# An explicit, state-free inverse of each 64-step triangle in an RWKV-7 and MLP kernel

## The chip, the cores and the metric

The kernel runs on one core of a Trainium2 chip. The metric is the device time of one execution in microseconds. All arithmetic is fp32.

## What is computed

An attention block with a recurrent state (RWKV-7) for 4 sequences, 8 heads, 768 steps and a head dimension of 40, followed by an MLP with a quick GELU on the 3072 resulting rows of 320 numbers. The reference, cut to what matters:

```python
for t in range(S):                                   # S = 768
    y[:, :, t] = einsum('bhd,bhde->bhe', r_t, state)
    Sa = einsum('bhde,bhe->bhd', state, a_t)
    state = state * w_t[:, :, None, :] - einsum('bhd,bhe->bhde', Sa, b_t) + einsum('bhd,bhe->bhde', v_t, k_t)
x = y.transpose(0, 2, 1, 3).reshape(3072, 320)
h = x @ w_in                                         # 320 x 2048
out = (h * sigmoid(1.702 * h)) @ w_out               # 2048 x 320
```

The kernel doesn't walk the steps. It takes 64 steps (a chunk) at once. Within a chunk, Sa at each step depends on Sa at the earlier steps of the chunk, which is a linear system with a unit triangular 64 x 64 matrix for each sequence and head: (I - N) X = B. N comes from a, b and the decay w alone; B has a part from v and k (A times v) and a part from the state that enters the chunk.

## The kernel before

**Units.** The work is cut into 24 units, numbered i: chunk c = i // 2 of twelve, and p = i % 2, a pair of sequences. A unit holds 2 sequences x 8 heads, so 16 triangles, eight on each half of the 128 partitions. Every product is made of four 64 x 64 tiles that run beside each other on the four quarters of TensorE (QUARTERS, helper mm at line 271, which is therefore the line of every matmul in the profile). An mm is two MATMUL and two LDWEIGHTS records.

**What happens in a unit.** decay (L476) makes the factors FT, GT and G from sums of log w. prep (L524) multiplies a, b and k by them and forms three score matrices: score_NT (L541, the transpose of N, masked to the upper triangle by L549), score_A (L554, masked by L562) and, times v, Av (L566, L574); score_RV (L578) is the same for r and v. solve (L605) then makes z, the decayed entering state (L614), and score_N (L618), whose product holds N (64 columns) and the state's part of B (40 columns) side by side; L630 masks the one, L633 adds Av to the other. Both go into the tile W, so from here on each step carries the state.

**The levels.** level (L665) is called for n = 0 to 5 and each of two halves b. For the late units (i of 4 and more) it runs Newton-like steps with a correction matrix E: the product has 104 columns (N and X), and for NT 64 more, and VectorE makes E (L707, L721, L716) while ScalarE or VectorE copies the product into the next W (L726). At the first level L705 subtracts from a tile called edge, which aside (L658) fills. The first four units (EARLY) use plain squaring, with an extra product by the identity in each level, and need E only at the end. The last level gives X for the tile M. sa_turned (L733) gives its transpose saT. The first two units have no entering state.

**The rest of a unit.** scores (L759) and read (L771) form the output y and the new state zraw (L788), which the unit i + 2 needs for its z. y is multiplied by FT (L812), goes to DRAM (L822) and comes back as xT (L826).

**MLP.** mlp (L834) has for each chunk 16 x 5 up tasks of 256 columns, a gelu on ScalarE for each pair of blocks (L847) and two times 8 down tasks of 320 columns. The weights arrive as float64 and are decoded to fp32 on VectorE and ScalarE by weight (L369 to L418) in eight pieces, in the first part of the run.

**What sets the order.** Everything is a task with a rank, a list of engines that can run it with a price for each, and the tiles that it reads, writes or needs room for. The class Plan (L59) orders all tasks ahead of time by a simulation with these prices: at each moment a free engine takes the task of lowest rank that is ready. Attention ranks by unit (10 i and about), weights have RANKS from 14 to 41, the MLP 10000 and more, so MLP products fill what attention leaves free on TensorE. The engines tried first are PE, ACT, DVE, POOL, in that order. Once written, the order on each engine is fixed. PSUM is four pairs of banks, and up and down hold at most one pair each. ak, b, W and E have two buffers, so one for each p.

Of the kernel before, what the change touches and what calls it, by code (L numbers as in the profile page):

```python
# [224 lines left out]
def rwkv7_gelu_quick(ctx: ExitStack, tc: tile.TileContext, time_d, v_d, w_d, wc_d, ak_d, b_d, rv_d, w_in, w_out, out):  # L225
# [11 lines left out]
    LEVELS = 6  # L237
# [13 lines left out]
    plan = Plan(dict(logw=3, wc=3, G=1, wch=3, wz=2, time=2, ak=2, b=2, rv=2, FT=3, GT=1, kh=2, bh=2, bz=2,  # L251
                     A=1, Av=1, RV=2, W=2, W0=2, W1=2, E=2, E0=2, E1=2, edge=1, zraw=2, zT=1, saT=1, M=2, y=1, x=1, xT=3, g=4, ob=1), 4)
# [72 lines left out]
    edge = single("edge", [128, 2, 2, 2, 168])  # L325
    for b, j in product(BITS, BITS):
        nc.vector.tensor_copy(edge[:, :, b, j, :64], ident.unsqueeze(1).to_broadcast([128, 2, 64]))
        nc.vector.tensor_copy(edge[:, :, b, j, 104:], ident.unsqueeze(1).to_broadcast([128, 2, 64]))
    twice = single("twice", [128, 64])
    nc.vector.tensor_add(twice, ident, ident)  # L330
# [14 lines left out]

    W_t, E_t = several("W", [128, 2, 2, 2, 168]), several("E", [128, 2, 2, 2, 128])

    ak_t, b_t, rv_t = several("ak", [128, 2, 8, 64]), several("b", [128, 8, 64]), several("rv", [128, 2, 8, 64])
    bz_t = several("bz", [128, 8 * 104 + 24])
    for t in bz_t:  # L350
        nc.gpsimd.memset(t[:, 8 * 104:], 0.0)
# [161 lines left out]
    Av_of = lambda i: buf("Av", i, [128, 2, 2, 2 * D])  # L513
    W_of = lambda s: W_t[s % 2]
    E_of = lambda s: E_t[s % 2]
# [6 lines left out]
    bz_of = lambda i: bz_t[i % 2][:, :8 * 104].rearrange("p (j n) -> p j n", n=104)  # L522

    def prep(i):  # L524
# [8 lines left out]
            bz_of(i)[:, :, :64], in0=b_of(i), scalar=-1.0, in1=GT_of(i), op0=ALU.mult, op1=ALU.mult),  # L533
                 reads=T("b", "GT"), writes=T("bz", "bhT"))
# [6 lines left out]
        def score_NT(t):  # L541

            ps = psum(t, "ps_NT")
            for b, f in product(BITS, BITS):
                for e, u in QUARTERS:
                    o, j = (2 * b + f) * 64, slot(b, u, f)
                    mm(ps[HALF[u], e, o:o + 64], bz_of(i)[HALF[e], j, :64], ahT()[HALF[e], j], o == 0)
        plan.add(R + 1, pe((4, 64)), score_NT, reads=T("bhT", "ahT"), uses=T("bz", "ak"), room=halves("W", first_w(i)), pair=("NT", i))
        plan.add(R + 1, dve(512), lambda t: nc.vector.tensor_tensor(  # L549
            W_of(first_w(i)).rearrange("p e b f n -> p e (b f) n")[:, :, :, 104:],  # L550
            psum(t, "")[:, :, :256].rearrange("p e (j t) -> p e j t", t=64), mask(upper), ALU.mult),
                 writes=halves("W", first_w(i)), pair=("NT", i))

        def score_A(t):  # L554

            ps = psum(t, "ps_A")
            for u, f in product(BITS, BITS):
                for e, b in QUARTERS:
                    o, j = (2 * u + f) * 64, slot(b, u, f)
                    mm(ps[HALF[b], e, o:o + 64], khT()[HALF[e], j], ahT()[HALF[e], j], o == 0)  # L560
# [5 lines left out]
        def times_v(t):  # L566

            ps, v_b = psum(t, "ps_Av"), time_of(i)[:, 2]
            for e, f in product(BITS, BITS):
                for b, u in QUARTERS:  # L570
                    o, h = (2 * e + f) * D, head(e, f, b, u)
                    mm(ps[HALF[u], b, o:o + D], A_of(i)[HALF[b], 4 * e + 2 * u + f], v_b[HALF[b], h * D:(h + 1) * D], o == 0)
        plan.add(R + 1, pe((4, 40)), times_v, reads=T("A", "time"), room=T("Av"), pair=("Av", i))
        plan.add(R + 1, any2(320), lambda t: copy(t.engine)(  # L574
            Av_of(i).rearrange("p e b n -> p b e n"), psum(t, "")[:, :, :160].rearrange("p b (e n) -> p b e n", e=2)),
# [18 lines left out]
    def first_w(i):  # L594
        return 2 * LEVELS * (i // 2) + i % 2

    def last_e(i):

        k, early = i // 2, EARLY // 2
        return 2 * (min(k, early - 1) + (LEVELS - 1) * max(k - early + 1, 0)) + i % 2  # L600

    def halves(name, n):
        return [(f"{name}{b}", n) for b in BITS]

    def solve(i):  # L605
# [4 lines left out]
        Av = lambda: Av_of(i).rearrange("p e b (f d) -> p e (b f) d", f=2)  # L610
        first = lambda: W_of(first_w(i)).rearrange("p e b f n -> p e (b f) n")

        if c > 0:
            plan.add(R, {"DVE": 490.0, "sbuf": True}, lambda t: nc.vector.tensor_mul(  # L614
                bz_of(i)[:, :, 64:], zraw_of(i - 2), wz_of(i).unsqueeze(2).to_broadcast([128, 8, D])),
                     reads=[("zraw", i - 2), ("wz", i)], writes=T("bz", "z"))

        def score_N(t):  # L618

            ps, n = psum(t, "ps_N"), 104 if c > 0 else 64  # L620
            for b, f in product(BITS, BITS):
                for e, u in QUARTERS:
                    o, j = (2 * b + f) * 104, slot(b, u, f)
                    mm(ps[HALF[u], e, o:o + n], ahT()[HALF[e], j], bz_of(i)[HALF[e], j, :n], o == 0)
        plan.add(R, pe((4, 104)), score_N, reads=T("ahT", "bhT", "Av") + (T("z") if c > 0 else []), uses=T("ak", "bz"),
                 room=halves("W", first_w(i)), pair=("N", i))

        def get(t):
            return psum(t, "")[:, :, :416].rearrange("p e (j n) -> p e j n", n=104)
        plan.add(R, dve(512), lambda t: nc.vector.tensor_tensor(first()[:, :, :, :64], get(t)[:, :, :, :64], mask(lower), ALU.mult),  # L630
                 writes=halves("W", first_w(i)), pair=("N", i))
        if c > 0:
            plan.add(R, dve(320), lambda t: nc.vector.tensor_add(first()[:, :, :, 64:104], get(t)[:, :, :, 64:], Av()),  # L633
                     reads=T("Av"), writes=halves("W", first_w(i)) + [("X", i)], pair=("N", i))

            def state_turned(t):

                ps, bz = psum(t, "ps_zT"), bz_t[i % 2]
                for u, b in product(BITS, BITS):
                    for e, f in QUARTERS:  # L640
                        o, at = (2 * u + b) * D, slot(b, u, f) * 104 + 64
                        mm(ps[HALF[f], e, o:o + D], bz[HALF[e], at:at + 64], ident[HALF[e], :D], o == 0)
            plan.add(R + 5, pe((4, 40)), state_turned, reads=T("z", "bhT"), uses=T("bz"), room=T("zT"), pair=("zT", i))
            plan.add(R + 5, any2(320), lambda t: copy(t.engine)(
                zT_of(i)[:, :DM].rearrange("p (r n) -> p r n", r=2), psum(t, "")[:, :, :160]), writes=T("zT"), pair=("zT", i))
        else:
            plan.add(R, any2(320), lambda t: copy(t.engine)(first()[:, :, :, 64:104], Av()), reads=T("Av"), writes=halves("W", first_w(i)))

        def signed(t, dst, src, done=False):

            if done:
                copy(t.engine)(dst, src)
            elif t.engine == "ACT":
# [4 lines left out]
        def aside(t):  # L658

            for u, e in QUARTERS:  # L660
                signed(t, edge[HALF[e], u, :, :, 64:104], W_of(first_w(i))[HALF[u], e, :, :, 64:104])
        if i >= EARLY:
            plan.add(R + 1, {"ACT": 4 * 330.0, "DVE": 4 * 330.0, "sbuf": True}, aside, reads=[("X", i)], uses=halves("W", first_w(i)), writes=T("edge"))

        def level(n, b):  # L665

            last = n == LEVELS - 1  # L670
            early = i < EARLY
            alone = n == 0 or early and not last
            s, es = first_w(i) + 2 * n, last_e(i) + 2 * (n - LEVELS + 1 if i >= EARLY else 0 if last else -1)

            def go(t):
                w, ps = W_of(s)[:, :, b], psum(t, "ps_level")
                E = None if alone else E_of(es)[:, :, b]
                lo = 0 if n < LEVELS - 2 else 64
                for j in BITS:
                    o = j * 208  # L680
                    for h, q in QUARTERS:
                        mm(ps[HALF[q], h, o + lo:o + 104], E[HALF[h], q, j, 64:] if E else w[HALF[h], q, j, 104:],
                           w[HALF[h], q, j, lo:104], j == 0)
                    if not last:
                        for h, q in QUARTERS:
                            mm(ps[HALF[q], h, o + 104:o + 168], E[HALF[h], q, j, :64] if E else w[HALF[h], q, j, :64],
                               w[HALF[h], q, j, 104:], False)
                if early and alone:
# [40 lines left out]
        for n in range(LEVELS):  # L729
            for b in BITS:  # L730
                level(n, b)
# [260 lines left out]
```

## Time and profile before

The median of three runs is 823.99 us (822.45 to 827.14). The profiled execution has a span of 816.7 us.

| operation | busy, us | instructions |
|---|---|---|
| ps_level products, by tile | 224 | 8768 MATMUL |
| up products | 274 | 3840 MATMUL |
| down products | 244 | 3072 MATMUL |
| y products | 42 | 1536 MATMUL |
| VectorE on level results (L705, L707, L716, L721, L726) | 189 | 292 |
| ScalarE copies W (L726) | 102 | 164 |

A tile's busy time counts the moments in which at least one of its matmuls was in flight. Matmuls of different tiles overlap, so the times of tiles add up to more than TensorE's busy time. The table of groups gives mean durations of single instructions[...]; the chain of work that ended last gives stretches from start to start and is the better place to read what a piece of TensorE work costs. [...]

### The profile page before, as it was taken

To read this page: it belongs to the slowest core of one execution; us is meant where nothing else is said; L and a number is where in the kernel's file an instruction comes from. 1 tells how busy PE (TensorE), PEld (TensorE's weight loads), DVE (VectorE), ACT (ScalarE), POOL (GpSimd) and SP (SyncE) were. 2 spreads that over 40 slices of the span, in tenths; PEclk is the share of its full clock that TensorE was granted. 3 is DMA by queue.
4 is the path that set the end of the run, shared out by engine and by line. 5 is a ranking of instruction groups with operands and counts; after the bars stand their busy time and mean duration, and the time that the engine had idled before them with its cause. 6 is when DMAs were issued, how large, how long until landed. Compare 5 with 4: busy or idle time off the path is not lost.

```text
span 816.7 us, 51357 instructions
## 1 busy us (share of the span) xinstructions
PE 749.6 (92%) x24192; PEld 636.1 (78%) x24192; DVE 477.7 (58%) x764; ACT 352.3 (43%) x603; POOL 153.3 (19%) x209
## 2 busy tenths in 40 slices
PE   4567887999999999999999989999999999999997
PEld 3556766787798888788888888887787887899785
DVE  7489778755755755756755654745556545455200
ACT  4376874444344253245254344355346345243210
POOL 4024052012202302302302302302103213200000
PEclk9899999999999999999999999999999999999999
DMA  9834452223403502412412512412403213110200
GB/s 348 329 110 146 136 194 72 70 69 89 134 17 91 152 20 86 133 45 82 138 45 68 152 44 74 141 46 72 142 15 98 71 50 92 40 33 4 60 10 18
DMA packets 32731, 76.31 MB, mean 93 GB/s; under 512 B 5096, under 2 KB 14312, under 8 KB 31496
## 3 DMA queue, kind: packets, MB, share of 16 engines
q1 hardware_dynamic: 32520, 73.03, 28.7%
q8 instruction: 190, 3.11, 1.6%
q14 instruction: 21, 0.17, 0.1%
HBM read 65.14 MB, written 7.86 MB: 89 GB/s over the span
## 4 chain that ended last, share of the span: by engine, by line
PE 79%; ACT 7%; DVE 6%; issue 4%; DMA 3%; SPq 1%; POOL 0%; ACTq 0%; DVEq 0%; POOLq 0%
PE ps_down L271 24%; PE ps_up L271 22%; PE ps_level L271 17%; PE ps_y L271 4%; PE ps_N L271 2%; ACT W L726 2%; PE ps_saT L271 1%; PE ps_Av L271 1%; PE ps_M L271 1%; PE ps_NT L271 1%; PE ps_A L271 1%; PE ps_RV L271 1%; PE ps_rz L271 1%; ACT L847 1%; PE ps_zT L271 1%
## 5 line engine op out<-in xcount | busy, mean ns | idle before, releaser
L271 PE MATMUL ps_up<-xT,w_sb 64*64 64x256 f32 x3840 | 274.5, 378 | 7.6 <-issue 4.5
L271 PE MATMUL ps_down<-w_sb,g 64*64 64x320 f32 x3072 | 243.8, 431 | 2.9 <-DVE w_sb L406 1.6
L726 ACT COPY W<-ps_level 128x672 f32<-128x672 f32 (+1 forms) x164 | 102.4, 626 | 184.2 <-PE ps_level L271 176.7
L271 PEld LDWEIGHTS ps_up<-xT,w_sb 64*64 64x64 f32 x3840 | 159.9, 134 | 27.3 <-issue 7.2
L271 PEld LDWEIGHTS ps_level<-W,E 64*64 64x64 f32 x5888 | 153.0, 134 | 27.9 <-issue 4.5
L271 PEld LDWEIGHTS ps_down<-w_sb,g 64*64 64x64 f32 x3072 | 130.9, 133 | 43.8 <-DVE w_sb L406 2.0
L271 PE MATMUL ps_level<-W,E 64*64 64x64 f32 (+2 forms) x5888 | 152.2, 230 | 7.8 <-issue 2.5
L721 DVE TENSOR_TENSOR E<-twice,ps_level 128x512 f32<-128x512 f32 x120 | 81.8, 686 | 87.8 <-ACT W L726 75.6
L538 POOL TENSOR_TENSOR kh<-time,G 128x320 f32<-128x320 f32 x23 | 20.8, 906 | 414.5 <-issue 289.3
L271 PE MATMUL ps_level<-W 64*64 64x64 f32 (+2 forms) x2560 | 69.4, 239 | 22.1 <-issue 10.3
L271 PEld LDWEIGHTS ps_level<-W 64*64 64x64 f32 x2560 | 66.2, 138 | 29.5 <-issue 15.0
L847 ACT ACTIVATE g<-ps_up 128x1024 f32<-128x1024 f32 x48 | 49.2, 1026 | 42.6 <-PE ps_up L271 42.2
L812 POOL TENSOR_TENSOR x<-y,FT 128x128 f32<-128x128 f32 x88 | 56.1, 667 | 0.7 <-DVE y L802 0.4
L705 DVE TENSOR_TENSOR W<-edge,ps_level 128x672 f32<-128x672 f32 x40 | 33.9, 850 | 12.2 <-PE ps_level L271 11.1
L530 POOL TENSOR_TENSOR ak<-ak,FT 128x512 f32<-128x512 f32 x20 | 27.9, 1394 | 64.1 <-DMA ak<-in_ak 55.8
L873 DVE TENSOR_TENSOR ob<-ob,ps_down 128x320 f32<-128x320 f32 x24 | 11.6, 482 | 48.0 <-ACT ob L871 45.7
L271 PE MATMUL ps_y<-RV,kh 64*64 64x104 f32 x768 | 37.1, 251 | 1.3 <-issue 1.3
L271 PE MATMUL ps_y<-M,bh 64*64 64x104 f32 x768 | 37.5, 250 | 0.5 <-issue 0.4
L726 DVE COPY W<-ps_level 128x672 f32<-128x672 f32 (+1 forms) x36 | 26.4, 733 | 14.2 <-PE ps_level L271 14.1
L271 PEld LDWEIGHTS ps_y<-RV,kh 64*64 64x64 f32 x768 | 29.0, 133 | 4.6 <-issue 2.9
L767 DVE TENSOR_TENSOR M<-ps_M,upper 128x512 f32<-128x512 f32 x24 | 16.6, 690 | 26.5 <-PE ps_M L271 26.4
L716 DVE TENSOR_TENSOR E<-twice,ps_level 128x256 f32<-128x256 f32 x40 | 16.8, 420 | 26.1 <-ACT W L726 16.9
(114 smaller groups left out, 986.0 us busy)
## 6 DMA issues: line engine op xcount, KB each, us to landing
time<-in_time SPq DMA_DIRECT2D x24, 480.0 KB
xT<-x_dram SPq DMA_DIRECT2D x48, 160.0 KB
ak<-in_ak SPq DMA_DIRECT2D x44, 160.0 KB
rv<-in_rv SPq DMA_DIRECT2D x44, 160.0 KB
wc<-in_wc SPq DMA_DIRECT2D x24, 264.0 KB
extra<-in_w_out SPq DMA_DIRECT2D x4, 1280.0 KB
logw<-in_w SPq DMA_DIRECT2D x24, 160.0 KB
RV<-in_v SPq DMA_DIRECT2D x24, 160.0 KB
```

The lines of the kernel that those rows point to most:

```text
L271: nc.tensor.matmul(o, lhsT, rhs, start=start, stop=True, skip_group_check=True)
L530: plan.add(R, {"DVE": 690.0, "POOL": 1270.0, "sbuf": True}, lambda t: of(t.engine).tensor_mul(ahT(), ahT(), FT_of(i)), reads=T("ak", "FT") ...
L538: plan.add(R + 4, {"POOL": 870.0, "DVE": 490.0, "sbuf": True}, lambda t, n=n, dst=dst: of(t.engine).tensor_mul(dst(i)[:, :, :D], by_head(t ...
L705: plan.add(key, dve(672), lambda t: nc.vector.tensor_sub(W_of(s + 2)[:, :, b], edge[:, :, b], item(t)[:, :, :, :168]), reads=T("edge"), wr ...
L716: plan.add(key, dve(256), lambda t: nc.vector.tensor_tensor(E_of(es + 2)[:, :, b, :, 64:], wide(ident if early else twice).to_broadcast([1 ...
L721: plan.add(key, dve(512), lambda t: nc.vector.tensor_sub(E_of(es + 2)[:, :, b].rearrange("p h j (n t) -> p h (j n) t", n=2), wide(twice).t ...
L726: plan.add(key, any2(4 * (168 - lo)), lambda t: copy(t.engine)(W_of(s + 2)[:, :, b, :, lo:], item(t)[:, :, :, lo:168]), writes=keeps, pair ...
L767: plan.add(R + 4, dve(512), lambda t: nc.vector.tensor_tensor(M_of(i)[:, :, :64].rearrange("p (e j) t -> p e j t", e=2), psum(t, "")[:, :, ...
L812: of(t.engine).tensor_mul(x[:, b ^ u, b], y_of()[:, at], FT_of(i)[:, at])
L847: plan.add(-45, act(1024), lambda t: nc.scalar.activation(g_of(c * NQ + q).rearrange("p m r n -> p r m n"), psum(t, "").rearrange("p r (m ...
L873: plan.add(-45, dve(320), lambda t: nc.vector.tensor_add(ob_of(serial), ob_of(serial), psum(t, "")[:, 1, :DM]), reads=[("ob", serial)], wr ...
```

## The change

The triangle's inverse is computed by itself, with no state in it, in a new function inverse, and applied to B at the end. The 64 x 64 triangle is seen as 32 x 32 blocks: the inverses of its two diagonal blocks are found by the levels, and the block below them follows from two more products. It is meant to take work off TensorE, and to keep the levels out of the path from state to state.

- **score_N** moves in front (rank 10 i - 5), with 64 columns and no state. Two predicated copies put its diagonal 32 x 32 blocks into E0, another copy saves the left columns in P21. score_NT, its mask, first_w, aside, the tile edge and the special treatment of the early units go.
- **Levels:** five in place of six, one task per level in place of two halves, for all units alike. A level is one product of 64 columns (32 in the last): the stationary operand EX holds the transpose of E in block-diagonal form, the moving one is W with two 32-column parts. VectorE makes the next E = 2 I - product. The stationary operand is no longer a second product: VectorE transposes E in 32 x 32 blocks into ES, and a multiplication by the mask quads (spread) makes EX of it on ScalarE (two calls), VectorE or GpSimd.
- **After the levels:** the inverse T is transposed and spread likewise. crossed copies the inverse across the partition halves into Tc. The products ps_Q and ps_T21 (32 columns) make the off-diagonal block, with a masked copy (QT) and a multiply-and-add on VectorE.
- **solve:** times_z makes the state's part of B (ps_Az, 40 columns) and an addition completes B. solved multiplies B by T (ps_X, 40 columns), sa_turned uses B and T. Both results are negated on ScalarE or VectorE.
- **Layout:** the rows of A and v change halves (time_tile of v is swapped), and z has a tile of its own.

```diff
-    LEVELS = 6
+    LEVELS = 5
+    WALK = "ebufbub"
...
+        def score_N(t):
...
+                    mm(ps[HALF[b], e, o:o + 64], ahT()[HALF[e], j], b_of(i)[HALF[e], j], o == 0)
+        plan.add(R, pe((4, 64)), score_N, reads=T("ahT", "bhT"), uses=T("ak", "b"), room=T("E0", "P21"), pair=("N", i))
+        for n in BITS:
+            plan.add(R, dve(256), lambda t, n=n: nc.vector.copy_predicated(
+                tiles_of(at(E0_t, i)), every(within_of(n), [128, 2, 4, 32]), blocks(psum(t, ""), 64)[:, :, :, 32 * n:32 * n + 32]),
...
+        def turned(rank, source, reads, n, dst, writes):
+
+            plan.add(rank, dve(256), lambda t: nc.vector.transpose(ES(n), source(t)), writes=[key("ES", n, 6)], **reads)
+
+            def spread(t):
+                if t.engine == "ACT":
+                    for h in BITS:
+                        nc.scalar.activation(dst[:, :, h], ES(n), ACT.Copy, scale=quads[:, h, :1])
+                else:
+                    of(t.engine).tensor_mul(dst, ES(n).unsqueeze(2).to_broadcast([128, 8, 2, 32]),
+                                            quads.unsqueeze(1).to_broadcast([128, 8, 2, 32]))
+            plan.add(rank, {"POOL": 1390.0, "DVE": 700.0, "ACT": 1000.0, "sbuf": True}, spread, reads=[key("ES", n, 6)], writes=writes)
...
+            def go(t):
+                ps, x, w = psum(t, "ps_level"), EX(n), at(W0_t, i) if first else W(n)
+                for k in range(4):
+                    for r, q in QUARTERS:
+                        mm(ps[HALF[q], r, k * wide:(k + 1) * wide], x[HALF[r], index(n, r, q, k)].rearrange("p n t -> p (n t)"),
+                           w[HALF[r], index(n, r, q, k), 64 - wide:], k == 0)
...
+            plan.add(rank, any2(512), lambda t: copy(t.engine)(tiles_of(W(n + 1)), blocks(psum(t, ""), 64)),
+                     writes=[key("W", n + 1, 5)], pair=pair)
+            plan.add(rank, dve(256), lambda t: nc.vector.tensor_sub(
+                tiles_of(E(n + 1)), every(two32, [128, 2, 4, 32]), blocks(psum(t, ""), 64)[:, :, :, :32]),
+                     writes=[key("E", n + 1, 5)], pair=pair)
+            turned(rank, lambda t: E(n + 1), dict(reads=[key("E", n + 1, 5)]), n + 1, EX(n + 1), [key("EX", n + 1, 5)])
...
+        plan.add(R + 3.5, pe((4, 32)), off_one, reads=T("P21", "T0"), room=T("QT"), pair=("Q", i))
...
+        plan.add(R + 3.5, pe((4, 32)), off_two, reads=T("Tc", "QT"), pair=("T21", i))
...
+            plan.add(R, pe((4, 40)), times_z, reads=T("ahT", "z", "Av"), uses=T("ak"), pair=("Az", i))
...
+        plan.add(R + 1, pe((4, 40)), solved, reads=T("T") + B, uses=T("B"), room=T("M"), pair=("X", i))
...
         prep(i)
+        inverse(i)
         solve(i)
```

## The prediction

> **What bounds the kernel now.** I read the page's busy shares and slices first. The reader is to see that TensorE is at nine tenths from the eighth slice (about 145 us) on, and that in front of that VectorE is the fullest engine.
>
> ```profile
> PE 749.6 (92%) x24192; PEld 636.1 (78%) x24192; DVE 477.7 (58%) x764; ACT 352.3 (43%) x603; POOL 153.3 (19%) x209
> PE   4567887999999999999999989999999999999997
> DVE  7489778755755755756755654745556545455200
> ```
>
> Then the table by stages, which splits the span into start, body and tail. Columns: stretch, its length, then busy us (instructions) of PE, PEld, DVE, ACT, POOL, then clock, DMA share and GB/s.
>
> ```profile
> 0.00:160.00 160.00, 115.30 (x4172) 97.79 (x4175) 122.69 (x164) 94.54 (x152) 45.74 (x62) 0.97 0.52 178
> 160.00:760.00 600.00, 582.16 (x19053) 499.11 (x19045) 350.09 (x590) 250.44 (x440) 107.55 (x147) 1.00 0.27 77
> 760.00:816.70 56.70, 52.14 (x996) 39.19 (x987) 4.92 (x11) 7.28 (x11) 0.00 (x0) 1.00 0.10 25
> ```
>
> The body idles 18 us in 600. In the start TensorE idles 45 us. The chain in order of time (start, us, what) says why, and gives unstretched prices where TensorE is full:
>
> ```profile
> 20.90 3.75 issue
> 63.92 1.96 DVE w_sb L396
> 104.99 6.95 DMA extra<-in_w_out
> 123.85 0.77 PE ps_level L271 x40
> 132.38 0.46 PE ps_M L271 x32
> 153.20 2.16 PE ps_down L271 x32
> 155.35 1.18 PE ps_level L271 x64
> 161.26 0.46 PE ps_level L271 x32
> 171.28 1.30 PE ps_up L271 x24
> 179.47 1.43 PE ps_y L271 x64
> ```
>
> The first three rows are the start's limits: gaps in which TensorE has nothing to wait for (DMA runs at 347 GB/s until 20 us, and the instructions come by DMA too), weight decoding on VectorE, and weight transfers. The others are prices. Half a level with 104 and 64 columns costs 0.59 us per 32 MATMULs; an early half with its identity product 0.77; a set of 32 MATMULs of at most 64 columns 0.46; y 1.43 per 64 (so 0.72 per 32 at 104 columns); up 54 ns and down 67.5 ns a MATMUL. Durations in the groups (223 to 431 ns) overlap, so I don't use them.
>
> Check of the prices on the body, from its counts by tile: up 3168 x 54 = 172; down 2352 x 67.5 = 159; levels of 19 units x 6.11 = 116; N 19 x 0.72 = 14; 4800 small ones x 14.4 ns = 69; y 1216 x 22.3 ns = 27; cum about 5. That is 561 of 600 us: the body runs at 0.935 of the prices. The same sum for the start is about 94 of 160, for the tail 52 of 57; 707 us in all.
>
> [...]the x32 level row mixes 40 and 64 columns and takes the same 0.46 as ps_M with 64. So 32-column products save nothing over 64. [...]L532 takes 679 ns at best and 1054 in the mean.
>
> **TensorE, part by part.** A late unit (20 of 24, from i = 4) now has 8 halves x 0.59 = 4.72, level 4 2 x 0.46 = 0.93, level 5 0.46, NT 0.46, N with the state's columns 0.72: 7.29 us, 416 MATMULs. Afterwards: N, five levels, Q, T21, Az, X, ten sets of 32 MATMULs x 0.46 = 4.64 us, 320 MATMULs. A, Av, saT, zT, M, y stay. Saved 2.65 x 20 = 53 us. An early unit has 8 x 0.77 + 2 x 0.60 + 0.46 = 7.82, plus NT and N: about 9.0 in place of 4.6 (the first two lack z, and so Az): 17.5 us over the four. Instructions fall as much as the work (24192 to about 21500 MATMULs), so fetching, [...], doesn't become the tighter bound.
>
> **Elementwise work.** These groups give the prices (busy, mean ns | idle before):
>
> ```profile
> L721 DVE TENSOR_TENSOR E<-twice,ps_level 128x512 f32<-128x512 f32 x120 | 81.8, 686 | 87.8 <-ACT W L726 75.6 <-PE ps_level L271 11.6
> L716 DVE TENSOR_TENSOR E<-twice,ps_level 128x256 f32<-128x256 f32 x40 | 16.8, 420 | 26.1 <-ACT W L726 16.9 <-PE ps_level L271 8.9
> L726 ACT COPY W<-ps_level 128x416 f32<-128x416 f32 x72 | 36.4, 506 | 73.7 <-PE ps_level L271 71.9 <-DVE E L716 1.1 <-DVE E L721 0.6
> L530 POOL TENSOR_TENSOR ak<-ak,FT 128x512 f32<-128x512 f32 x20 | 27.9, 1394 | 64.1 <-DMA ak<-in_ak 55.8 <-ACT FT L493 6.3 <-DMA logw<-in_w 2.0
> ```
>
> Removed per late unit on VectorE: NT and N masks 1.37, N add 0.48, L705 and L707 3.07, L721 6 x 0.686 = 4.12, L716 0.84: 9.9 us; on ScalarE W copies 2.9 + 2.0, edge 1.3, M 0.6: 6.8. Added and bound to VectorE: six transposes, two predicated copies, four E, T21's sum, 13 x 0.42, and Az's add 0.48: 5.9. Transposes and predicated copies are in no row: from below 0.42 [...], from above 0.84 if they run at half rate; I take 0.42, the high end adds 3.4. Shared out: four W copies 0.59, crossed, QT, P21, M about 2.3, W0 0.42, and six spreads, each 0.75 on ScalarE (two calls), 0.69 on VectorE or 1.39 on GpSimd: about 9.6. So 15.5 for 16.7, moved from VectorE to ScalarE and GpSimd, which are at 0.42 and 0.18 in the body. I cost it at nothing there: MLP matmuls hide it. The loss of the state from the levels costs nothing either: the inverse can run while the former chunk's state is finished.
>
> The new wait is the hop at each level: product, E, transpose, spread, next product. Ready to ready it is 0.46 + about 0.3 handing over + 0.42 + 0.42 + 0.75 to 2.1 (a GpSimd spread held up by half) + 0.15 = 2.5 to 3.9 us, so 19 to 25 us for a unit with both ends. Queued behind a waiting level product are MLP pieces of 0.4 to 1.1 us on TensorE; behind a spread on ScalarE the gelu (1.03), for which the MLP waits. Two units run beside each other, and the body takes about 63 us per two, so the chain fits.
>
> **The start** is where elementwise time counts. An early unit had about 2.7 us bound to VectorE (its levels needed only W copies) and now has 5.9 plus its part of the spreads, some 4 to 6 more; four to five units make 15 to 25 us, of which the 37 us that VectorE idles there can take the larger part. Against it stand 17.5 us less matmul work and 11% fewer instructions in the stretch with fetch gaps. I put the net at 5 us gained, with bounds of 20 lost to 15 gained.
>
> **Sum.** Body: 53 / 0.935 = 57 us. With the start's 5: 824 - 62 = 762 us.
>
> **Rivals.** (a) More: the start gains 13, and the body's efficiency rises to 0.96 since attention stops waiting on its state: (561 - 50) / 0.935 - 511 / 0.96 = 14 more. 762 - 8 - 14 = 740. For it: fewer, shorter state-bound steps; against it: only some 18 us of idling are left to win. (b) Less: VectorE's extra work lies on the weight decoding (15 lost, not 5 gained) and the efficiency falls to 0.91 as the fixed order meets wrong prices: 762 + 20 + 15 = 797. For it: VectorE at 77% in the start, unknown prices. (c) Slower: the hop takes over as bound. Per unit some 25 hops on four engines; if each also waits 1.5 us behind gelus, decodes and MLP pieces, a unit takes 25 + 38 = 63 us, and Tc and QT, single buffers, let the two units block each other: 66 us for a chunk x 12 + 48 for first loads and last MLP = 840. For it: static in-order queues; against it: 4 idle tenths on VectorE, 6 on ScalarE.
>
> **Numbers.** 762: 0.60; (a) 0.17; (b) 0.12; (c) 0.11. The range 736 to 800 takes in both (a) and (b) and leaves out (c) and the far end of (a). Faster by over 0.5%: 0.60 + 0.17 + 0.12 = 0.89, less 0.01 for a (b) gone further: 0.88; same 0.02; slower 0.10.
>
> **What would show it.** Right: about 21500 MATMULs, PE slices still at 9 from about 150 us, x32 level products at 0.46, transposes near 0.42 us, VectorE below 58% in the body, GpSimd and ScalarE up. Wrong: slices of PE at 6 to 8 in the body with levels idle behind spreads or transposes (c); weights decoded well after 146 us (b); transposes or predicated copies at 0.8 us and more.

## The result, and the profile after

The changed kernel takes 774.61 us in the median of five runs (771.52 to 776.12), beside 822.45 us of the kernel before on the same chip (820.88 to 827.14): a ratio of 0.9395, with an interval of 0.936 to 0.9431, so 47.8 us less. The prediction was 762 us; the time lies inside its range, and 14 of the 62 us that it expected to gain did not come. A repeat of both gave 0.9415 (0.9371 to 0.9459), so in what follows the changed kernel stands at 0.9405 of the kernel before, the mean of the two. Single executions over 1.5 per cent slower than the fastest of the same kernel (three of the kernel before, and one of four of the last kernel below, at 772 us) are left out of all ratios. Line numbers of the changed kernel are one higher in the matmul helper (L272 for L271) and some 14 to 35 higher further down.

The page of the kernel after begins with the busy shares, and the slices of the span follow:

```profile
PE 695.3 (90%) x21504; PEld 579.1 (75%) x21504; DVE 456.5 (59%) x821; ACT 377.4 (49%) x696; POOL 212.7 (28%) x269
PE   3566885898999999989999999999999999999997
DVE  8999898757647556556537556356666646433100
PEclk9577897999999999989999999999999999999999
```

TensorE has 2688 matmuls fewer (21504 for 24192) and 54 us less busy time, but its share of the span fell too, from 92 to 90 per cent. The first seven slices of VectorE are now nearly full (8999898 for 7489778), and the row PEclk has half-speed stretches in the same place (577 and a 7), where the kernel before has 9899999. The table by stages says where the time went. Columns: stretch, its length, busy us (instructions) of PE, PEld, DVE, ACT, POOL, then clock, DMA share, GB/s.

```profile
0.00:160.00 160.00, 110.47 (x3525) 88.30 (x3529) 139.01 (x212) 94.59 (x178) 63.80 (x83) 0.84 0.52 180
160.00:715.00 555.00, 534.76 (x17139) 453.97 (x17135) 313.27 (x600) 277.01 (x510) 148.87 (x186) 0.99 0.29 83
715.00:769.70 54.70, 50.12 (x863) 36.84 (x853) 4.22 (x10) 5.80 (x8) 0.00 (x0) 0.99 0.09 23
```

The limit at 715 us is chosen so that the body does the same MLP and attention work as 160 to 760 us did before: 3168 up matmuls against 3194 counted now, 2352 down against 2353, and 1216 of y in both. So the body gained 45 us (600 to 555), the tail 2 us, and the start nothing at all, although its matmul work fell as well. At the prediction's own prices the work of the three stages is now 82.0, 512 and 50.3 us, where it was 99.6, 563 and 52.4. (The prediction's own sum had 94 for the start before; the counts by tile give 99.6.) The body runs at 512 / 555 = 0.922 of the prices, where it ran at 563 / 600 = 0.938; the start saved 17.6 us of priced work for no time.

The chain of waits of the kernel after in order of time (start, us, what), to be held beside the lines shown of before:

```profile
140.38 1.39 DVE w_sb L420
141.81 1.31 PE ps_down L272 x16
...
145.59 1.43 PE ps_y L272 x64
...
333.37 2.58 issue
...
417.68 0.46 PE ps_level L272 x32
418.14 1.30 PE ps_up L272 x24
```

Three things are to be seen. The prices hold: 0.46 us for 32 small products, 1.30 for 24 up matmuls, 1.43 for 64 of y, all as before. The start still ends with the decoding of the last weights on VectorE, at 141.8 us; before, it ended at 141.5 (1.63 us from 139.84 on). And the body has a gap of 2.58 us in which TensorE waits for nothing that the profile shows.

Three groups of the new elementwise work (line, engine, operation, out<-in, count | busy, mean ns | idle before it, and what ended most of it):

```profile
L633 ACT ACTIVATE EX<-ES,quads 128x256 f32<-128x256 f32 x150 | 68.0, 501 | 62.8 <-DVE ES L628 62.4
L628 DVE STREAM_TRANSPOSE ES<-E 128x256 f32<-128x256 f32 x120 | 53.1, 444 | 5.7
L635 POOL TENSOR_TENSOR EX<-ES,quads 128x512 f32<-128x512 f32 x19 | 27.9, 1469 | 59.0 <-DVE ES L628 48.9
```

The transpose takes 444 ns, near the lower end that the prediction took. The spread on ScalarE takes two calls of 501 ns, but the second begins before the first has ended: 68.0 us for 75 pairs, so 0.91 us where 0.75 was taken. The durations of these 150 calls add up to 75 us, so that here they are not quite their costs.

### The profile page after: what moved, and what is told of

The parts are those of the page before. It is cut to its first block, busy times and chain, and to the rows that moved or that the text cites. A ratio compares the mean times of both kernels' runs of the same rounds, so it can differ in the third digit from the quotient of the medians.

```text
span 769.7 us, 46087 instructions
## 1 busy us (share of the span) xinstructions
PE 695.3 (90%) x21504; PEld 579.1 (75%) x21504; DVE 456.5 (59%) x821; ACT 377.4 (49%) x696; POOL 212.7 (28%) x269
## 4 chain that ended last, share of the span: by engine, by line
PE 76%; DMA 7%; DVE 7%; ACT 5%; issue 3%; SPq 1%; POOL 1%; ACTq 0%; DVEq 0%; POOLq 0%
PE ps_up L272 25%; PE ps_down L272 25%; PE ps_level L272 6%; PE ps_y L272 4%; DMA logw<-in_w 2%; PE ps_M L272 1%; ACT g L882 1%; PE ps_T L272 1%; PE ps_Av L272 1%; PE ps_X L272 1%; PE ps_saT L272 1%; PE ps_Q L272 1%; PE ps_RV L272 1%; DMA x_dram<-x 1%; PE ps_N L272 1%
## 5 line engine op out<-in xcount | busy, mean ns | idle before, releaser
L272 PE MATMUL ps_up<-xT,w_sb 64*64 64x256 f32 x3840 | 264.6, 385 | 8.3 <-DMA xT<-x_dram 2.7
L272 PE MATMUL ps_down<-w_sb,g 64*64 64x320 f32 x3072 | 250.5, 434 | 5.3 <-DVE w_sb L420 2.8
L272 PEld LDWEIGHTS ps_up<-xT,w_sb 64*64 64x64 f32 x3840 | 161.7, 136 | 35.5 <-issue 6.9
L272 PEld LDWEIGHTS ps_down<-w_sb,g 64*64 64x64 f32 x3072 | 135.1, 134 | 45.9 <-issue 5.3
L272 PEld LDWEIGHTS ps_level<-W,EX 64*64 64x64 f32 x3840 | 89.4, 142 | 36.4 <-issue 14.2
L272 PE MATMUL ps_level<-W,EX 64*64 64x64 f32 (+1 forms) x3840 | 91.9, 228 | 21.4 <-issue 5.8
L633 ACT ACTIVATE EX<-ES,quads 128x256 f32<-128x256 f32 x150 | 68.0, 501 | 62.8 <-DVE ES L628 62.4
L664 ACT COPY W<-ps_level 128x512 f32<-128x512 f32 x69 | 40.4, 586 | 108.3 <-PE ps_level L272 106.7
L666 DVE TENSOR_TENSOR E<-two,ps_level 128x256 f32<-128x256 f32 x96 | 39.8, 415 | 44.9 <-ACT W L664 44.7
L628 DVE STREAM_TRANSPOSE ES<-E 128x256 f32<-128x256 f32 x120 | 53.1, 444 | 5.7
L623 POOL TENSOR_TENSOR W<-two,E 128x256 f32<-128x256 f32 x22 | 16.0, 728 | 103.9 <-DVE E L617 103.9
L635 POOL TENSOR_TENSOR EX<-ES,quads 128x512 f32<-128x512 f32 x19 | 27.9, 1469 | 59.0 <-DVE ES L628 48.9
L547 POOL TENSOR_TENSOR ak<-ak,GT 128x512 f32<-128x512 f32 x24 | 39.0, 1624 | 6.1 <-DMA ak<-in_ak 3.2
L272 PE MATMUL ps_y<-RV,kh 64*64 64x104 f32 x768 | 36.1, 250 | 1.8 <-DVE M L803 1.1
L272 PE MATMUL ps_y<-M,bh 64*64 64x104 f32 x768 | 36.0, 250 | 0.2 <-issue 0.2
L272 PEld LDWEIGHTS ps_y<-RV,kh 64*64 64x64 f32 x768 | 28.6, 133 | 5.7 <-DVE M L803 3.2
L664 DVE COPY W<-ps_level 128x512 f32<-128x512 f32 x27 | 18.6, 687 | 23.8 <-PE ps_level L272 23.7
```

Of the source, the lines that this page charges most:

```text
L272: nc.tensor.matmul(o, lhsT, rhs, start=start, stop=True, skip_group_check=True)
L547: plan.add(R, {"DVE": 690.0, "POOL": 1270.0, "sbuf": True}, lambda t: of(t.engine).tensor_mul(khT(), khT(), GT_of(i)), reads=T("ak", "GT") ...
L623: plan.add(R, {"DVE": 430.0, "POOL": 750.0, "sbuf": True}, lambda t: of(t.engine).tensor_sub(at(W0_t, i)[:, :, :32], two32.unsqueeze(1).to ...
L628: plan.add(rank, dve(256), lambda t: nc.vector.transpose(ES(n), source(t)), writes=[key("ES", n, 6)], **reads)
L633: nc.scalar.activation(dst[:, :, h], ES(n), ACT.Copy, scale=quads[:, h, :1])
L635: of(t.engine).tensor_mul(dst, ES(n).unsqueeze(2).to_broadcast([128, 8, 2, 32]), quads.unsqueeze(1).to_broadcast([128, 8, 2, 32]))
```

## The experiments

All times are compared as ratios to the kernel before on the same chip; a difference to the changed kernel is the ratio less 0.9405, times some 818 us, and is known to about 4 us. An edit also changes the prices in the plan, and with them the order of all tasks, so that small differences say nothing: two edits below that leave TensorE's work alone moved the time by -2 and by 3.6 us. Four questions were asked: what bounds the body now, whether the new chain of elementwise hops holds it, where the start's gain went, and whether either can be mended.

### What bounds the body: columns or instructions

The late units' level products were issued a second time (same columns, twice the instructions).

```diff
-                for k in range(4):
+                for k in (0, 1, 2, 3) * (1 if last or i < EARLY else 2):
```

> Each product of levels 0 to 3 of the late units is issued twice (the second overwrites the first): 80 more tasks of 32 MATMULs, so 80 x 0.46 = 37 us of TensorE work and 5120 more instructions (12%). If TensorE's work as priced sets the time: 37 / 0.92 = 40 us more, about 815. If the supply of TensorE instructions sets it (the body then scales with the count, 34300 + 5100): some 80 us more, about 855. If the elementwise hops of the levels set it: at most 10 more, about 785.

The ratio is 1.019 (1.0148 to 1.0232): 64 us more than the changed kernel. These are 20 x 4 x 32 = 2560 more matmuls with as many weight loads, so 25 ns for each pair, where the price of such a product is 0.46 / 32 = 14.4 ns. By estimate, streaming alone would have cost 37 us (80 x 0.46), and a time in proportion to the instructions some 80. So the added columns alone don't explain it.

The second kernel streams 112 columns instead of 64 in the same products, with no more instructions:

```diff
-                        mm(ps[HALF[q], r, k * wide:(k + 1) * wide], x[HALF[r], index(n, r, q, k)].rearrange("p n t -> p (n t)"),
-                           w[HALF[r], index(n, r, q, k), 64 - wide:], k == 0)
+                            mm(ps[HALF[q], r, k * 112:(k + 1) * 112], x[HALF[r], index(n, r, q, k)].rearrange("p n t -> p (n t)"),
+                               flat[HALF[r], j:j + 112], k == 0)
```

> The products of levels 0 to 3 of the late units stream 112 columns in place of 64, 48 of them unused: the count of instructions is as before the edit, TensorE's work grows by 80 x 0.31 = 24 us (112 columns at 22.4 ns a MATMUL x 112 / 104, so 0.77 us for 32 in place of 0.46). If TensorE's work as priced sets the time: 24 / 0.92 = 27 us more, about 801. If the supply of instructions sets it: 0 to 5 more, about 777. If the elementwise hops set it: the 0.31 us lie in each of 80 hops, two chains beside each other, 12 more at most.

It takes 0.9423 (0.938 to 0.9465): 1.5 us more, so nothing that can be told from zero, where some 26 us of streaming were added, by an estimate from the price of the up products (48 columns at 54 / 256 = 0.21 ns, 2560 times). Its table by stages (columns as above) and its timeline (start, us, what, tile shape, partitions and columns, count) show where they went:

```profile
160.00:715.00 555.00, 547.14 (x17252) 466.63 (x17248) 301.58 (x581) 291.13 (x545) 145.69 (x180) 1.00 0.28 83
```

```profile
446.93 0.97 PE L272 MATMUL ps_level<-W,EX 64*64 64x112 f32 x32
447.69 0.65 PE L272 MATMUL ps_Q<-T,P 64*64 64x32 f32 x32
```

From start to start the widened level takes 0.76 us, for 0.46 with 64 columns, so the added streaming is really paid where TensorE is full. What it replaced is idling and slow stretches: TensorE is busy 547 us of the same 555, where the changed kernel was busy 535, and the mean clock is 1.00 for 0.99. The kernel with doubled products has its price at such a place too, 0.93 us for 64 matmuls, or 14.5 ns each:

```profile
413.68 1.15 PE L272 MATMUL ps_level<-W,EX 64*64 64x64 f32 x64
414.61 2.38 PE L272 MATMUL ps_up<-xT,w_sb 64*64 64x256 f32 x40
```

So a single pair isn't held to 25 ns. The rest of its 64 us are gaps and slowed stretches elsewhere. In the profile's table of waits, from 160 to 700 us, TensorE idles for "issue" (it waits for nothing that the profile shows) 19.4 us in the doubled kernel, 7.2 in the changed one and 2.3 in the widened one.

The third kernel does two of the four groups of stationaries of these products, each with 128 columns: the same columns with 1280 matmuls fewer. Half of the levels' results are left out.

```diff
+                if less:
+                    for k in range(2):
+                        for r, q in QUARTERS:
+                            j = min(index(n, r, q, k), 6)
+                            mm(ps[HALF[q], r, k * 128:(k + 1) * 128], x[HALF[r], index(n, r, q, k)].rearrange("p n t -> p (n t)"),
+                               w[HALF[r], j:j + 2].rearrange("p j t -> p (j t)"), k == 0)
+                    return
```

> The products of levels 0 to 3 of the late units use 2 of their 4 groups of stationary blocks, each with 128 columns in place of 64: as many columns streamed, half the instructions (80 x 32 = 2560 fewer); half of the level's products are left out. On the chip of the first four runs the changed kernel would be at 0.9395 x 816.2 = 767. If the supply of instructions bounds the body, at the 12.7 ns an instruction that the doubled products showed (65 us for 5120): 32 us less, a ratio of 0.90. If TensorE's streaming bounds it: 2 us less, 0.937. If the hops do: within 3 us.

It takes 0.9196 (0.9157 to 0.9236), 17 us less: half of what a pure limit by instructions was to give, and far more than the 2 us of a limit by columns. That is 13 ns for each pair of matmul and weight load, against 25 when pairs were added. So the count of instructions weighs beside the columns, and neither sets the time alone.

What was it before? In the kernel before, four kinds of small products (A, RV, M, rz) were given 128 columns instead of 64, with no more instructions:

```diff
-                    mm(ps[HALF[u], f, o:o + 64], rv[HALF[f], 1, j], rv[HALF[f], 0, j], o == 0)
+                    mm(ps[HALF[u], f, o:o + 128], rv[HALF[f], 1, j], flat(rv)[HALF[f], 64 * j:64 * j + 128], o == 0)
```

> The kernel before with the products A, RV, M and rz streaming 128 columns in place of 64 (the further 64 unused, result unchanged): no more instructions, 94 tasks x 0.41 us (128 columns at 55 ns for two passes of four tiles in place of 29 ns, by the rate of the 104-column products) = 39 us more streaming on TensorE. If the kernel before was bound by the supply of instructions too, as the changed one is by the widened level products: 0 to 6 us slower, ratio 1.00 to 1.007. If its body was bound by TensorE's streaming: 39 / 0.94 = 41 us slower, ratio 1.05; a half of that would speak for a balance of both.

It takes 1.0335 (1.0261 to 1.0409), 27 us more for an estimated 39 us of added streaming. So before the change added columns cost about 0.7 of their price, and after it 1.5 us of 26. This is a difference of degree, with two reservations: the two experiments widen different products, though of the same kind (sets of 32 matmuls with 64 columns), and to different widths, 128 and 112. The kernel before idles for "issue" as much as the changed one, 7.8 us, and its widened form idles less, 3.0. No products were doubled in it. That the change moved the body from a bound by streaming to one by the number of instructions is therefore not shown.

Can instructions be saved elsewhere? The down products of the changed kernel were issued as one 128x128 tile instead of four quarters: 2304 matmuls fewer.

```diff
-                        for r, b in QUARTERS:
-                            o = p * 128 + b * 64
-                            mm(po[HALF[b], r, :DM], g[HALF[r], f % 2, o:o + 64], w_out_sb[HALF[r], f * DM:(f + 1) * DM], f == 0)
+                        mm(po[:, f % 2, :DM], g[:, f % 2, p * 128:(p + 1) * 128], w_out_sb[:, f * DM:(f + 1) * DM], f < 2)
```

> The same arithmetic and result as the changed kernel, but each down product is one 128 x 128 tile in place of four 64 x 64 ones: 3072 MATMULs become 768, 4608 instructions fewer, the time to stream 320 columns the same. If the supply of instructions bounds the body: 4608 x 12.7 ns = 58 us less, cut off where streaming takes over (the body's priced work is 512 of 555 us), so 30 to 43 less, ratio 0.885 to 0.905. If TensorE's streaming bounds it: no change (0.94). [...]

It takes 0.9701 (0.966 to 0.9741): 24 us more. The timeline shows why:

```profile
400.68 0.69 PE L272 MATMUL ps_level<-W,EX 64*64 64x64 f32 x32
...
401.31 1.34 PE L272 MATMUL ps_down<-w_sb,g 128*128 128x320 f32 x4
...
402.58 0.69 PE L272 MATMUL ps_A<-ak 64*64 64x64 f32 x32
```

From start to start the level takes 0.63 us (0.46 beside other quarters) and the down task 1.27 (16 x 67.5 ns = 1.08 in quarters): 0.36 us for going to the other tile shape and back. The same with the up products as two 64x128 tiles, 1920 matmuls fewer:

```diff
-                for r, h in QUARTERS:
-                    mm(ph[HALF[h], r, m * 256:(m + 1) * 256], w_in_sb[HALF[r], 2 * q + m, k, h * 64:(h + 1) * 64], x[HALF[r]],
-                       m == 0 and k == 0)
+                for r in BITS:
+                    mm(ph[:, r, m * 256:(m + 1) * 256], w_in_sb[HALF[r], 2 * q + m, k], x[HALF[r]], m == 0 and k == 0)
```

> Same arithmetic and result as the changed kernel. An up task is two 64 x 128 tiles in place of four 64 x 64 ones: 3840 MATMULs become 1920, 3840 instructions fewer, columns streamed as before. If the supply of instructions is what bounds the body and the array takes the other shape without a pause: at 7.3 ns an instruction (the halved products) 28 us less, ratio 0.905. If each going between shapes costs as it did with the 128 x 128 down tiles (about 0.36 us there and back), up tasks being as many as down tasks or more: 10 to 40 us slower than the changed kernel, 0.95 to 0.99.

It takes 1.0039 (1.0012 to 1.0065), and 821.4 us against 770.4 of the changed kernel repeated beside it: 51 us more. Its timeline:

```profile
382.39 1.13 PE L272 MATMUL ps_up<-xT,w_sb 64*128 64x256 f32 x8
...
383.46 0.69 PE L272 MATMUL ps_rz<-rv,zT 64*64 64x64 f32 x32
...
384.08 0.70 PE L272 MATMUL ps_up<-xT,w_sb 64*128 64x256 f32 x4
```

The small task takes 0.62 us from start to start, and one up task 0.63 (384.08 to 384.71, where the next small task starts) instead of 8 x 54 ns = 0.43: again 0.36 us for there and back. Two up tasks in a row take 1.07 us (382.39 to 383.46), so the second costs 0.44, its price in quarters: the time is lost at the change, not in the larger tile. There are 480 up tasks and 192 down tasks, so the loss is larger. What fewer instructions would bring the MLP can't be seen through this cost, and these two kernels say nothing on the limit.

### The chain of hops

In the late units each transpose was done twice, 0.44 us more on every hop and 53 us more on VectorE:

```diff
+            def transposed(t):
+                for _ in range(1 if i < EARLY else 2):
+                    nc.vector.transpose(ES(n), source(t))
```

> Each 32 x 32 transpose of the late units is done twice: 120 x 0.44 = 53 us more on VectorE, and each hop 0.44 us longer. If elementwise work is hidden in the body (mine): within 4 us of the changed kernel, about 775. If hops or VectorE bound the body: 25 to 50 more, 800 to 825.

It takes 0.9379 (0.9344 to 0.9414), 2 us less, within the uncertainty of no change. Its body:

```profile
160.00:715.00 555.00, 536.44 (x17394) 449.45 (x17390) 349.43 (x704) 291.56 (x540) 145.04 (x182) 1.00 0.28 83
```

VectorE is busy 349 us for 313 (the plan gave some of its other work to ScalarE, which has 292 for 277), and TensorE is as full as before. The hops have room, and this added elementwise work cost nothing.

The spreads were then bound to ScalarE, whose calls take 501 and 502 ns in the two groups of the changed kernel, where GpSimd's spreads take 1.27 to 1.47 us:

```diff
-            plan.add(rank, {"POOL": 1390.0, "DVE": 700.0, "ACT": 1000.0, "sbuf": True}, spread, reads=[key("ES", n, 6)], writes=writes)
+            plan.add(rank, {"ACT": 1000.0}, spread, reads=[key("ES", n, 6)], writes=writes)
```

> The spreads all go to ScalarE (two calls, 1.0 us together, by the trace of the changed kernel) and none to VectorE or GpSimd: VectorE and GpSimd are relieved of 20 and 42 us, of which about a sixth lies in the start. If VectorE's load bounds the start: 3 to 6 us faster, about 770. If it doesn't: within 2 us of 774.6. If hops set the pace in the body, the shorter spread (1.0 in place of up to 1.5 us) gives 5 or more.

It takes 0.9449 (0.94 to 0.9498), 3.6 us more, not to be told from no change. Which engine spreads makes no difference that can be seen in the whole.

### The start

Four microseconds of VectorE work for each of the eight pieces of weights were left out, in the kernel before and in the changed one alike:

```diff
-        plan.add(rank, {"DVE": one, "sbuf": True}, bounded, reads=T("magnitude"), writes=T("bounded"))
-        plan.add(rank, {"DVE": one + two, "sbuf": True}, exponent, reads=T("bounded"), writes=T("exponent"))
-        plan.add(rank, {"DVE": one, "sbuf": True}, significand, reads=T("exponent"), writes=T("significand"))
-        plan.add(rank, act(PIECE), fraction, reads=T("significand"), writes=T("fraction"))
+        plan.add(rank, act(PIECE), fraction, reads=T("magnitude"), writes=T("fraction"))
```

Of the kernel before:

> The kernel before with three of the steps of the weight decoding left out (bounded, exponent, significand: 4.0 us on VectorE per piece, 8 pieces). If VectorE's decoding bounds the start of both kernels: the kernel before gains 5 to 12 us (ratio about 0.99), the changed one more. If loads or the first chunk's chain bound the start: within 3 us for both.

Of the changed kernel:

> The changed kernel with the same three decoding steps left out. VectorE was 87% busy in its start against 77% before. If the decoding on VectorE swallowed what the start should have gained: 15 to 25 us less than the changed kernel (ratio about 0.915), and the gap to the kernel before, treated alike, grows from 48 to 56 to 65 us. If the start is bound by loads: the gap stays at 48.

The kernel before takes 1.0002 of its own time (0.9977 to 1.0027): nothing gained. The changed kernel takes 0.9247 (0.9194 to 0.9299): 13 us gained. The first 160 us of the two, before_light ahead of after_light:

```profile
0.00:160.00 160.00, 119.52 (x4150) 105.36 (x4153) 99.34 (x150) 80.27 (x131) 37.25 (x55) 0.93 0.52 179
```

```profile
0.00:160.00 160.00, 119.92 (x3964) 103.25 (x3968) 122.14 (x207) 96.34 (x168) 74.94 (x96) 0.89 0.54 189
```

Before, 4150 matmuls with the lighter decoding and 4172 without: VectorE's decoding did not hold TensorE back there. After, 3964 against 3525: 439 matmuls more in the same time, which at the body's 555 / 17139 = 32.4 ns a matmul are 14 us, the whole gain. So the decoding became a bound of the start through the change. What held the start before isn't known: with 23 us less on VectorE (122.69 to 99.34) it didn't move.

Last, an edit that takes VectorE's new work out of the start without leaving anything out: in the first six units the spreads, the copies of W and P21 and the crossed copy go to ScalarE alone, and the first W to GpSimd.

```diff
-            plan.add(rank, {"POOL": 1390.0, "DVE": 700.0, "ACT": 1000.0, "sbuf": True}, spread, reads=[key("ES", n, 6)], writes=writes)
+            plan.add(rank, {"ACT": 1000.0} if i < 6 else {"POOL": 1390.0, "DVE": 700.0, "ACT": 1000.0, "sbuf": True}, spread, reads=[key("ES", n, 6)], writes=writes)
...
-            plan.add(rank, any2(512), lambda t: copy(t.engine)(tiles_of(W(n + 1)), blocks(psum(t, ""), 64)),
+            plan.add(rank, act(512) if i < 6 else any2(512), lambda t: copy(t.engine)(tiles_of(W(n + 1)), blocks(psum(t, ""), 64)),
```

> Same arithmetic and result as the changed kernel. For the first six units spreads, W copies, P21 and crossed may run on ScalarE alone and W0 on GpSimd alone, so that VectorE has some 10 us less to do while it decodes the weights. If VectorE's load in the start holds the kernel back (leaving decoding steps out gave 15 us): 5 to 11 us less than the changed kernel, ratio 0.926 to 0.934. If what counted was the length of the decoding's own chain: within 2 us of it, as ScalarE now delays its part of the decoding.

It takes 0.9257 (0.9223 to 0.9291), 756.4 us in the median against 770.4 of the changed kernel repeated beside it, and so is faster than both kernels. That repeat was the control:

> The changed kernel once more, as the base for the two runs beside it and for the earlier ones: ratio 0.9395 to the kernel before, within its interval of 0.936 to 0.943.

0.9415 (0.9371 to 0.9459). The 13 us are as many as those of the lighter decoding. Where its TensorE fills up wasn't seen in a profile, so that the two gains have the same cause is likely and not shown.

## Why the prediction was right, and where it was off

**Direction and main term: right.** The late units' matmul work was to fall by 53 us, and at the same prices the body and the tail hold 51 + 2 = 53 us less. The prices that this rests on were found again after (0.46, 1.30, 1.43 us). That a set of 32 columns costs as much as one of 64 was inferred before from sets of 40; after, a set of ps_Q with 32 columns takes 0.47 us from start to start (331.86 to 332.33). About 21500 matmuls were forecast, and 21504 ran. That the levels left the path from state to state, the other aim of the change, shows no gain of its own, since the body's efficiency did not rise.

**Elementwise work costs nothing in the body: right.** VectorE is at 313 / 555 = 56 per cent, under the 58 named, ScalarE at 50 and GpSimd at 27. Doubling the transposes changed nothing measurable. With this the slower rival (c), the hop chain as bound, falls: 0.44 us more on every hop would have shown. The prices that no row of before showed were the author's estimates: 0.42 us came out close for the transpose (444 ns) and the predicated copy (443 ns), and 0.75 us was low for ScalarE's spread, which took 0.91 in two calls of 501 ns. The error lay in slack and cost nothing in the body.

**"Body: 53 / 0.935 = 57 us": this step failed.** The prediction turned 53 us of work into 57 us of time by the efficiency of before (0.935), on the ground that instructions fall as much as work does, so that fetching doesn't become the tighter bound. The body and the tail gained 47. The ground held in the mean: in the body matmuls fell by 10 per cent (19053 to 17139), priced work by 9 (563 to 512), and TensorE idles for "issue" as much as before (7.2 us for 7.8). What failed is that the efficiency stays. It fell from 0.938 to 0.922, and 512 / 0.938 would have been 546 us in place of 555. Most of these 9 us are seen in the records at two places, as a gap and as half-clock stretches. The table by windows shows the worse of the two:

```profile
332.00:336.00 4.00, 1.40 (x78) 1.15 (x71) 0.80 (x2) 2.58 (x7) 2.67 (x2) 0.93 0.92 283
336.00:340.00 4.00, 3.86 (x105) 3.64 (x108) 2.56 (x6) 0.00 (x0) 0.00 (x0) 0.50 0.25 86
```

The timeline of that place has seven small tasks in a row, from 328.47 us on, the last of which holds the gap of the chain:

```profile
332.33 0.68 PE L272 MATMUL ps_Az<-z,ak 64*64 64x40 f32 x32
...
333.04 0.33 PE L272 MATMUL ps_level<-W,EX 64*64 64x64 f32 x3
...
335.94 1.01 PE L272 MATMUL ps_level<-W,EX 64*64 64x64 f32 x27 [2.58 <-issue]
```

The level product stops after 3 of 32 matmuls, though its inputs are there, and the others come 2.6 us later, while the DMA engines are at 0.92; after that the clock stands at 0.50. The profile of the repeat has the same stop in the same product:

```profile
336.72 1.01 PE L272 MATMUL ps_level<-W,EX 64*64 64x64 f32 x27 [2.85 <-issue]
```

In the changed kernel the mean clock is 0.50 in 336 to 340 us and 0.71 in 340 to 344, so by estimate it stood at half for some 7 us behind the gap of 2.58 us. Whether the gap brought it about was not shown. By mean clock, 0.97 in 260 to 360 us and 0.98 in 360 to 460 (1.00 in the body of before), it cost, by estimate, 3 + 2 = 5 us, and the gap itself 2.6. In the bodies of the kernels with doubled transposes and with all spreads on ScalarE, which have the same products in another order, the mean clock is 1.00, and up to 715 us they had done 2474 and 2448 down matmuls, where the changed kernel had done 2353 and its repeat 2356. (The second has a gap for "issue" of 2.5 us too, without the slow clock.) So this loss seems to belong to the order in which the tasks came to lie. Single profiles show it; in the whole times it lies within the uncertainty.

Why the gap opens isn't settled. The profile's table of queues has the instructions as transfers of 16 KB; there are 169 for TensorE's 43008 matmuls and weight loads, so about 254 in each:

```profile
q8 instruction: 169, 2.77, 1.6%
```

(columns: transfers, MB, share of the engines; 190 before, for 48384, so again about 254). In 160 to 700 us they came 4.12 us apart after, 4.05 before, and 3.96 with the products issued twice, so the mean spacing after wasn't the closest possible: the shortage of instructions, if it is one, is local, behind several small tasks in a row. Whether the transfers or the issue of the instructions set a limit, if either did, was not told apart, as every experiment changed both counts together.

**The start's +5 us: wrong in size, by the term named as uncertain.** The 15 to 25 us of added VectorE work were right in amount (122.69 to 139.01 us busy, so 16), but "of which the 37 us that VectorE idles there can take the larger part" failed. The added operations stand in one order with the decoding on VectorE, which was full from the first slices on: the last weight is ready at 141.8 us for 141.5, and 17.6 us less matmul work bought nothing. The lighter decoding shows it, with 13 us gained after and none before, and moving the work to ScalarE and GpSimd gives as much back. The place is the wait for the last weights. From 120 to 140 us, in the kernel before, the changed kernel, and the changed kernel with the lighter decoding:

```profile
120.00:140.00 20.00, 16.21 (x677) 13.44 (x680) 16.07 (x21) 10.56 (x16) 3.73 (x4) 1.00 0.26 83
```

```profile
120.00:140.00 20.00, 11.43 (x332) 7.89 (x324) 19.14 (x28) 11.29 (x23) 1.70 (x1) 0.74 0.06 23
```

```profile
120.00:140.00 20.00, 19.65 (x652) 14.23 (x649) 12.60 (x25) 8.60 (x19) 5.81 (x9) 1.00 0.24 70
```

The changed kernel runs half the matmuls of the kernel before, with VectorE full and hardly any transfers; with the lighter decoding, whose last weight is ready at 112.5 us, this is gone. The lost 17.6 us are idling only for a smaller part. In the first 160 us TensorE idles 50 us for 45; the other 13 us are matmuls that take longer, busy 28 us above the priced work (110.5 for 82.0), before 16, at a mean clock of 0.84 for 0.97 (0.89 with the lighter decoding). Whether the low clock has to do with the waits for VectorE was not shown.

Rival (b) had this mechanism and put it at 15 us lost; here it took the gain of the matmuls and no more. Of the 15 us missing in the profile, 5 are the start's and 10 the body's and the tail's.

**Rival (a)** needed an efficiency of 0.96 and 13 us from the start. The start could have given them, as the edit to the first six units shows; the body stayed at 0.922.

## What to carry to other kernels

Before dividing saved work by the efficiency of before, ask what the lost time consists of. Here work and instructions fell alike, and the efficiency fell all the same, in good part through one gap behind small products (2.6 us) and the slow clock seen after it and at a second place (5 us together, by estimate), while in two other orders of the same products the clock stayed full. Test what bounds a stretch with one kernel that adds columns and one that adds instructions, and read in their traces whether the added time lies in the products or in gaps between them. And price new elementwise work by stage: what is free in the body can hold up the start, where the same engine prepares the weights, so give an operation with a choice of engines another choice there.

## What the runs showed of the hardware that was not expected

- Widening the 64-column products of the changed kernel to 112 columns cost 1.5 us for an estimated 26 us of streaming, though each widened set of 32 took 0.76 us for 0.46; in the kernel before, 64 to 128 columns cost 27 us for an estimated 39.
- A change of the tile shape between tasks took about 0.36 us there and back, the same for a 128x128 tile and for 64x128 tiles among 64x64 ones. With it 2304 matmuls fewer came with 24 us more, and 1920 fewer with 51 us more.
- In the changed kernel a gap of 2.58 us in an already thinly used stretch was followed by a clock of 0.50 in the next 4 us and 0.71 in the 4 after them. The repeat has a gap of 2.85 us in the same product, and the same mean clock of 0.97 in 260 to 360 us.
- GpSimd's spread of 512 elements took 1.27 to 1.47 us and VectorE's 0.73 to 0.75, by group; ScalarE, with two overlapping calls of 0.50, took 0.91.
